# Attention and a Strassen MLP on one core: w_out's operand sums in place and two groups to a load, w_in's stores a round later, and another way to finish the last quarter

## Chip, cores, metric

The kernel runs on one NeuronCore of a Trainium2 chip. The metric is device microseconds (us) for one execution. The kernel before takes 911.48 us, the median of 8 runs (909.97 to 914.7).

## What is computed

A hashed attention feeds a two-layer MLP with a PReLU-like activation:

```python
# q, k, v: (4, 8, 768, 64); proj: (64, 6)
mask   = q_bucket[:, :, :, None] == k_bucket[:, :, None, :]   # sign bits of q @ proj and k @ proj
scores = where(mask, q @ k.T / 8, -1e9)
attn   = softmax(scores) @ v                                  # (4, 8, 768, 64)
x = attn.transpose(0, 2, 1, 3).reshape(3072, 512)
h = x @ w_in                                                  # w_in (512, 2048)
g = maximum(h, 0) + alpha * minimum(h, 0)
out = g @ w_out                                               # w_out (2048, 512), out (3072, 512)
```

## The kernel before

**Two paths.** `fast_path` computes everything and a flag; `general_path` runs only if the flag is set, which it is not here. Almost every instruction of an engine is put into a written-out order with `do(...)`. The DMA starts are not: a scheduler places them in the queue of SP (SyncE) by its own estimate of when they are due, and SP then takes them strictly in that order, so a DMA start that waits for a semaphore holds up all that are behind it.

**Attention** runs over 32 units (`u`), two for each of 16 pairs of heads, about 10.4 us each. A unit makes scores (`sc`), exponentials (`pt`), the product with v (`av`), the row sums (`sm`) and the quotient `x`, which goes to DRAM (`x_s`). Every second unit `turn` (line 669) transposes the next pair's q and k (`tp_q`, `tp_k`), whose tiles `qn` and `kn` are loaded by L500, and `vn` by L489. Beside that the weights are read (`raw`, L567), brought to shape, and grouped: `weight_group` stores finished groups of w_out into `w_out_r` and queues, for each of four groups of w_in, four sums (`one`, L638) and a store (`store`, L643: four DMA starts of 448 KB into `w_in_s`). `weight_sums(1)` takes one queued sum per unit, and the store at once behind the fourth sum.

**The MLP** is done by Strassen's scheme (Winograd's form: seven products instead of eight), two levels. For each of 4 batches there are 8 blocks `ff1` (`f_0` to `f_7`, tiles of w_in called `wi`) and 7 blocks `ff2` (`z_1` and so on, tiles of w_out called `wl`). Within a block PE does seven products in the order 1, 2, 5, 6, 3, 7, 4 (`Product.step`, banks a, b, c), and step 1 of the next block is put ahead of step 4 of this one, so PE's queue reads: step 1 of block n+1, step 4 of block n, steps 2, 5, 6, 3, 7 of block n+1, step 1 of block n+2, and so on. The tile `wi` of block n+2 (`load_w`, L827, two buffers) can be loaded only once step 4 of block n is done, and is needed at step 1 of block n+2.

**w_out's operand sums** are made in the first batch, beside its `ff1` blocks, in the two buffers that later hold `wl`. `load_out(n)` (L932) loads the four raw quarters of group n (512 KB) into the lower half of an eight-slot tile `wo`; `sum_out(n)` (L937) has VectorE (DVE) make four sums into the upper half, stores these (L938, 512 KB, into `w_out_s`) and calls `load_out(n + 2)`, which has to wait for that store to land since it reuses the tile. The loop over blocks `j` (L1147) calls `sum_out` for groups (0), (1, 2), (3), (4, 5), (6), (7) in the blocks j = 0 to 5, between the step 7 and the step 4 of that block. At j = 4 `largest` and `verdict` (L1034 to L1050) make the flag; PE has four tiny transposes there (`vd`).

**The end.** `ff2` adds the last product (p = 4) to the first (`m_1`). Its quarter "21" comes straight from PSUM: ScalarE (ACT) copies it (L980), DVE adds `m_1` (L974). `turn_last` (L1015) then transposes the last two output tiles on PE, copies them from PSUM on ACT (L1023) and stores them (L1025): `turn_last(0)` through SP, `turn_last(1)` in two parts through ACT's own DMA queue.

Of the kernel before, what the change touches and what calls it, by code (L numbers as in the profile page):

```python
# [8 lines left out]
F32 = mybir.dt.float32  # L9
# [3 lines left out]
ALU = mybir.AluOpType  # L13
# [393 lines left out]
def fast_path(  # L407
# [12 lines left out]
    nc = tc.nc  # L420
    P = 128
    B, H, S, D = q.shape
    NB = proj.shape[1]
    NTOK, DM = out.shape
# [6 lines left out]
    CH = 3  # L431
# [10 lines left out]
    do = tc.keep_in_program_order  # L442
    PE, DVE, ACT, POOL = nc.tensor, nc.vector, nc.scalar, nc.gpsimd
# [11 lines left out]
    out_v = out.rearrange("(b p c) d -> b c p d", p=P, c=NC)  # L455


    ident = const.tile([P, P], F32, name="ident")
# [12 lines left out]
    w_out_r = dram.tile([4, P, NI, DM // 2], F32, name="w_out_r")  # L471
    w_out_s = dram.tile([4, P, NI, DM // 2], F32, name="w_out_s")
# [149 lines left out]
    sums_due = []  # L622
# [25 lines left out]
        sums_due.append((store, ()))  # L648

    def weight_sums(count):  # L650
        while sums_due and (count or sums_due[0][0].__name__ == "store"):
            fn, x = sums_due.pop(0)
            count -= fn.__name__ == "one"
            fn(*x)


    def two_banks(name):
        return psum.tile([P, 2, 512], F32, name=name, tag="sc", bufs=3)
# [255 lines left out]
    H2, HK, HC = DM // 4, NI // 2, CW // 2  # L914
    w2, g2, m2, to_turn = {}, {}, {}, []

    def load_w2(b, n):

        if n < 7:
            t = late[0].tile([P, NI, 2 * H2], F32, name=f"wl{b}_{n}", tag="wl")  # L920
            m = SIDES[ORDER[n]][0]
            nc.sync.dma_start(t, w_out_r[m] if m < 3 else w_out_s[m - 3])
            for m, kh, dh in ((0, 0, 0), (1, 1, 0), (2, 1, 1), (21, 0, 1)):
                w2[b, n, m] = t.rearrange("p n (f i) -> p n i f", i=2)[:, kh * HK : (kh + 1) * HK, dh]

    w_o = {}

    def load_out(n):

        if n < NI:  # L930
            w_o[n] = late[0].tile([P, 8, DM // 2], F32, name=f"wo{n}", tag="wl")
            nc.sync.dma_start(w_o[n][:, :4], w_out_r[:, :, n].rearrange("m p d -> p m d"))  # L932

    def sum_out(n):
        w = w_o[n]
        for to, x, op, y in ((4, 3, ALU.add, 2), (6, 0, ALU.subtract, 3), (5, 4, ALU.subtract, 0), (7, 1, ALU.subtract, 5)):
            do(DVE.tensor_tensor(w[:, to], w[:, x], w[:, y], op=op))  # L937
        nc.sync.dma_start(w_out_s[:, :, n].rearrange("m p d -> p m d"), w[:, 4:])  # L938
        load_out(n + 2)

    def sides_g(b, n):
        t = g_m[b, SIDES[ORDER[n]][1]]
        for m, kh, ch in ((0, 0, 0), (1, 1, 0), (2, 1, 1), (12, 0, 1)):
            g2[b, n, m] = t[:, kh * HK : (kh + 1) * HK, ch * HC : (ch + 1) * HC]

    def sum_w2(b, n, *ms):

        if n < 7:
            for m in ms:
                x, op, y = {  # L950
                    3: (21, ALU.add, 2), 4: (3, ALU.subtract, 0), 5: (0, ALU.subtract, 21), 6: (1, ALU.subtract, 4),
                }[m]
                w2[b, n, m] = t = late[0].tile([P, HK, H2], F32, name=f"ws{b}_{n}_{m}", tag=f"ws{m}", bufs=1 + (m < 5))
                do(DVE.tensor_tensor(t, w2[b, n, x], w2[b, n, y], op=op))  # L954

    def sum_g2(b, n, *ms):

        if n < 7:
            for m in ms:
                x, y = {3: (12, 0), 4: (2, 3), 5: (2, 12), 6: (1, 4)}[m]  # L960
                g2[b, n, m] = t = late[0].tile([P, HK, HC], F32, name=f"gs{b}_{n}_{m}", tag=f"gs{m}", bufs=1 + (m < 5))
                do(DVE.tensor_tensor(t, g2[b, n, x], g2[b, n, y], op=ALU.subtract))  # L962

    def ff2(b, n):

        p = ORDER[n]
        acc = late[0].tile([P, 2, CW], F32, name=f"m{b}_{p}", tag={1: "m1", 5: "m5"}.get(p, "m"), bufs=1 if p in (1, 5) else 3)
        m2[b, p] = acc

        def add(to, x, *quarter):  # L970
            t, x = m2[b, to], m2[b, x]
            if quarter:
                t, x = (a[:, quarter[0], quarter[1] * HC : (quarter[1] + 1) * HC] for a in (t, x))
            do(DVE.tensor_tensor(t, t, x, op=ALU.add))  # L974

        def finish(c, x, more):
            i, jj = int(c[0]) - 1, int(c[1]) - 1
            dst = acc[:, i, jj * HC : (jj + 1) * HC]
            if more is None:
                do(ACT.copy(dst, x))  # L980
            else:
                do(DVE.tensor_tensor(dst, x, more, op=ALU.add))
            if p == 4:
                add(4, 1, i, jj)
            if c == "21":

                for to, x in {2: [(2, 1)], 6: [(1, 6)], 3: [(3, 5), (3, 1)], 7: [(1, 7), (5, 1)]}.get(p, []):
                    add(to, x)
                done = {2: (2, 0, 0), 3: (3, 0, 1), 7: (5, 1, 1), 4: (4, 1, 0)}.get(p)
                if done:  # L990
                    to_turn.append((b, *done))

        return Product(
            f"z{b}_{p}", HC, HK, lambda m, k: w2[b, n, m][:, k], lambda m, k: g2[b, n, m][:, k], finish,
        )

# [16 lines left out]
    def turn_last(n):  # L1013

        b, p, half, ch = to_turn.pop(0)  # L1015
        o = late[0].tile([P, CH, P, 2], F32, name=f"o_{p}", tag=("o", "m5")[n], bufs=2 - n)
        for ts in ((2,), (0, 1)) if n else ((0, 1, 2),):
            ps = two_banks(f"to{p}").rearrange("p a f -> p (a f)").rearrange("p (t i f) -> p t i f", i=2, f=P)
            for i in range(2):
                for t in ts:  # L1020
                    do(PE.transpose(ps[:, t, i], m2[b, p][:, i, t * P : (t + 1) * P], ident))
            ts = slice(ts[0], ts[-1] + 1)
            do(ACT.copy(o[:, ts].rearrange("p t f i -> p t i f"), ps[:, ts]))  # L1023
            dst = out_v[b, ch * CH : (ch + 1) * CH].rearrange("c p d -> p c d")
            (nc.scalar if n else nc.sync).dma_start(  # L1025
                dst[:, ts, half * 2 * P : (half + 1) * 2 * P], o[:, ts].rearrange("p t f i -> p t (f i)"),
            )


    top = const.tile([P, 4], F32, name="top")  # L1030
# [2 lines left out]
    def largest():  # L1033
        do(DVE.tensor_reduce(top[:, :2], mags, axis=mybir.AxisListType.X, op=ALU.max))  # L1034
        do(DVE.tensor_reduce(top[:, 2:3], wmax, axis=mybir.AxisListType.X, op=ALU.max))
        do(DVE.tensor_reduce(top[:, 3:4], alpha, axis=mybir.AxisListType.X, op=ALU.max))
# [102 lines left out]
    late = []  # L1139
    attn.close()  # L1140
    late.append(ctx.enter_context(tc.tile_pool(name="late", bufs=2)))
    load_out(0)
    load_out(1)
    blocks = [(b, what, n) for b in range(B) for what, count in (("1", NI), ("2", 7)) for n in range(count)]


    for j, (b, what, n) in enumerate(blocks):  # L1147
        n2 = n + 1 if what == "2" else 0 if n == NI - 1 else 7
        if n2 == 0:
            sides_g(b, 0)  # L1150
            sum_w2(b, 0, 3, 4)
        now.step(2) if j else now.step(6)
        if j == 0:
            now.step(3)
            now.step(7)
            now.step(2)
        now.step(22)
        if j == 4:
            largest()
        if 0 < n2 < 7:  # L1160
            sides_g(b, n2)
            sum_w2(b, n2, 3, 4)
        if n2 < 7:
            sum_g2(b, n2, 3, 4)
        if j:
            now.step(5)
            now.step(6)
            now.step(3)
            sum_w2(b, n2, 6)
            now.step(7)  # L1170
            sum_w2(b, n2, 5)
            sum_g2(b, n2, 5)
        if j == 4:
            verdict()
        for n_out in [(0,), (1, 2), (3,), (4, 5), (6,), (7,)][j] if j < 6 else ():
            sum_out(n_out)
        if what == "1":
            load_w(b * NI + n + 2)
            if n >= NI - 2:
                load_w2(b, n - NI + 2)  # L1180
        else:
            load_w2(b, n + 2)
            if b + 1 < B:
                if n == 0:
                    load_x(b + 1)
                if n == 6:
                    for m in range(4):
                        sum_x(b + 1, m, DVE)
        if j + 1 < len(blocks):
            turn_out()  # L1190
        else:
            turn_last(0)
        before = now
        if j + 1 < len(blocks):
            b1, what1, n1 = blocks[j + 1]
            now = ff1(b1, n1) if what1 == "1" else ff2(b1, n1)
            now.step(1)
        before.step(4)
        if n2 < 7:
            sum_g2(b, n2, 6)  # L1200
# [29 lines left out]
```

## Time and profile before

| what | us |
|---|---|
| median of 8 runs | 911.48 |
| the profiled execution, its whole time | 913.63 |
| its span, first to last instruction | 911.8 |
| PE (TensorE) busy | 888.5 (97%) |
| VectorE (DVE) busy | 756.1 (83%) |
| ScalarE (ACT) busy | 410.5 (45%) |
| attention, up to the first `ff1` product | 0 to 352.9 |
| first batch's `ff1` blocks | 352.9 to 432.0 |
| last matmul product ends, span ends | 903.5, 911.8 |

The mean granted clock of TensorE is 0.996 of full speed over the span. HBM moves 146 GB/s over the span; in the stretch from 355 to 425 us, where w_out's sums are made, 232 GB/s. "L848" is line 848 of the kernel; tiles are given by their names without numbers. PE is busy nearly all the time, so the few stretches in which it is not are what there is to read; a busy share of another engine says little by itself.

### The profile page before, as it was taken

To read this page: it belongs to the slowest core of one execution; us is meant where nothing else is said; L and a number is where in the kernel's file an instruction comes from. 1 tells how busy PE (TensorE), PEld (TensorE's weight loads), DVE (VectorE), ACT (ScalarE), POOL (GpSimd) and SP (SyncE) were. 2 spreads that over 40 slices of the span, in tenths; PEclk is the share of its full clock that TensorE was granted. 3 is DMA by queue.
4 is the path that set the end of the run, shared out by engine and by line. 5 is a ranking of instruction groups with operands and counts; after the bars stand their busy time and mean duration, and the time that the engine had idled before them with its cause. 6 is when DMAs were issued, how large, how long until landed. Compare 5 with 4: busy or idle time off the path is not lost.

```text
span 911.8 us, 15639 instructions
## 1 busy us (share of the span) xinstructions
PE 888.5 (97%) x5885; PEld 590.9 (65%) x5885; DVE 756.1 (83%) x1353; ACT 410.5 (45%) x735; POOL 88.3 (10%) x178
## 2 busy tenths in 40 slices
PE   7999999999999999989999999999999999999996
PEld 3444444444444445546998556998556998556996
DVE  4888898988998997887889667989667989768985
ACT  6888888888888873222111222111222112222111
POOL 1222222222223221000000000000000000000000
PEclk9999999999999999999999999999999999999999
DMA  8787887698788764767333534333535333531242
GB/s 219 188 203 167 212 214 202 171 259 230 172 226 201 181 170 143 242 221 267 132 112 114 159 119 155 128 116 112 164 113 168 115 129 98 173 103 40 93 141 72
DMA packets 138053, 146.88 MB, mean 161 GB/s; under 512 B 78304, under 2 KB 126192, under 8 KB 134384
## 3 DMA queue, kind: packets, MB, share of 16 engines
q1 hardware_dynamic: 127248, 132.42, 47.0%
q0 software_dynamic: 8704, 12.58, 8.6%
q8 instruction: 48, 0.79, 0.4%
q10 hardware_dynamic: 2016, 0.79, 0.3%
q14 instruction: 37, 0.30, 0.1%
HBM read 104.87 MB, written 28.31 MB: 146 GB/s over the span
## 4 chain that ended last, share of the span: by engine, by line
PE 56%; DMA 4%; DVE 2%; POOL 0%; ACT 0%; issue 0%; SPq 0%; DVEq 0%; ACTq 0%; POOLq 0%
PE f_6a L848 2%; PE z_4a L848 2%; PE z_6a L848 2%; PE z_7a L848 2%; PE z_3a L848 2%; PE z_5a L848 2%; PE z_2a L848 2%; PE z_1a L848 2%; PE f_7a L848 2%; PE f_0a L848 2%; PE f_1a L848 2%; DMA w_out_s<-wo 2%; PE f_5a L848 2%; PE f_2a L848 2%; PE f_4a L848 2%; PE f_3a L848 2%
## 5 line engine op out<-in xcount | busy, mean ns | idle before, releaser
L733 ACT ACTIVATE pt<-sc 128x768 f32<-128x768 f32 x192 | 152.7, 813 | 49.5 <-PE sc L728 47.3
L728 PE MATMUL sc<-qT,kT 64*128 64x384 f32 x768 | 155.1, 482 | 0.0
L761 PE MATMUL av<-pt,vn 128*32 128x384 f32 (+1 forms) x1536 | 130.6, 488 | 2.8 <-DVE x L802 2.7
L761 PEld LDWEIGHTS av<-pt,vn 128*32 128x32 f32 x1536 | 46.6, 109 | 78.4 <-issue 68.9
L728 PEld LDWEIGHTS sc<-qT,kT 64*128 64x128 f32 x768 | 68.1, 188 | 34.4 <-issue 34.2
L898 DVE TENSOR_TENSOR g<-g,g 128x384 f32<-128x384 f32 x128 | 68.4, 555 | 2.2
L728 PE MATMUL sc<-qb,kb 64*128 64x384 bf16 x384 | 63.0, 324 | 2.5 <-ACT kb L716 1.0
L743 POOL DMA_DIRECT2D accp<-pt x32 | 38.5, 1204 | 188.9 <-issue 101.0
L962 DVE TENSOR_TENSOR gs<-g,gs 128x768 f32<-128x768 f32 x56 | 53.4, 953 | 1.0
L962 DVE TENSOR_TENSOR gs<-g 128x768 f32<-128x768 f32 x56 | 53.3, 952 | 0.0
L954 DVE TENSOR_TENSOR ws<-wl 128x512 f32<-128x512 f32 x56 | 38.5, 688 | 17.7 <-DMA wl<-w_out_s 16.5
L894 DVE SCALAR_TENSOR_TENSOR g<-h,alpha 128x384 f32<-128x384 f32 x32 | 19.7, 617 | 29.2 <-ACT h L887 29.2
L728 PEld LDWEIGHTS <-kb 64*128 64x128 bf16 x384 | 19.4, 94 | 34.2 <-issue 12.1
L705 ACT ACTIVATE qb<-hs,hb 32x384 bf16<-32x384 f32 x62 | 35.6, 574 | 1.1
L748 DVE TENSOR_TENSOR accd<-accd,pt 128x768 f32<-128x768 f32 x32 | 30.7, 958 | 3.3
L751 DVE TENSOR_TENSOR accd<-accd,accp 128x768 f32<-128x768 f32 x32 | 30.7, 958 | 2.8 <-DMA accp<-pt 1.7
L799 DVE STREAM_TRANSPOSE dn<-rr 128x384 f32<-128x384 f32 x32 | 18.5, 578 | 17.4 <-POOL rr L797 17.4
L742 DVE TENSOR_TENSOR accp<-pt,pt 128x768 f32<-128x768 f32 x32 | 30.4, 952 | 2.0 <-ACT pt L733 2.0
L747 DVE TENSOR_TENSOR accd<-pt,pt 128x768 f32<-128x768 f32 x32 | 30.4, 949 | 0.4 <-ACT pt L733 0.4
L974 DVE TENSOR_TENSOR m<-m,m 128x768 f32<-128x768 f32 (+1 forms) x40 | 28.4, 709 | 1.9 <-ACT m L980 1.2
L797 POOL COPY rr<-rr 32x6 f32<-32x6 f32 x64 | 27.6, 431 | 2.6
L716 ACT ACTIVATE kb<-hs,hb 64x384 bf16<-64x384 f32 (+1 forms) x47 | 27.2, 578 | 0.6
(334 smaller groups left out, 1794.4 us busy)
## 6 DMA issues: line engine op xcount, KB each, us to landing
wi<-w_in_s SPq DMA_DIRECT2D x32, 896.0 KB, 4.9
wl<-w_out_s SPq DMA_DIRECT2D x16, 1024.0 KB, 4.8
accp<-pt POOLq DMA_DIRECT2D x32, 384.0 KB, 5.1
wl<-w_out_r SPq DMA_DIRECT2D x12, 1024.0 KB, 4.9
raw<-in_moe_w_out_dram SPq DMA_DIRECT2D x16, 512.0 KB, 4.8
raw<-in_moe_w_in_dram SPq DMA_DIRECT2D x16, 512.0 KB, 4.4
w_in_s<-wsi SPq DMA_DIRECT2D x16, 448.0 KB, 5.2
vn<-in_v_dram SPq DMA_DIRECT2D x16, 384.0 KB, 6.3
```

The lines of the kernel that those rows point to most:

```text
L705: do(ACT.activation(bits["q", pi][D * s : D * s + 32, cols], ps["q"][c : c + 32, half, :CW], AF.Sign, bias=hb[c : c + 32],))
L728: do(PE.matmul(sc[:, s, :CW], what["k", pi][r, ks], what["q", pi][r, qs], start=first, stop=not first,))
L733: do(ACT.activation(pt[:, :, :CW], sc[:, :, :CW], AF.Exp, scale=SCALE / DOWN))
L742: do(DVE.tensor_tensor(accp[u], p(u, 0), p(u, 1), op=ALU.add))
L743: nc.gpsimd.dma_start(accp[u], p(u, 2), accum_op=ALU.add)
L748: do(DVE.tensor_tensor(accd[u], accd[u], p(u, 5), op=ALU.add))
L751: do(DVE.tensor_tensor(accd[u], accd[u], accp[u], op=ALU.add))
L761: do(PE.matmul(av[u][D * s + t : D * s + t + 32, :w], nat["v", pi][:, s, kc * D + t : kc * D + t + 32], prob[u, kc][:, s, :w], start=(kc = ...
L848: do(PE.matmul(self.ps[bank], self.left(left, k), self.right(right, k), start=start and k == 0, stop=k == self.nk - 1, skip_group_check=no ...
L898: do(DVE.tensor_tensor(new_g(b, to)[:, i], g_m[b, x][:, i], g_m[b, y][:, i], op=ALU.subtract))
L954: do(DVE.tensor_tensor(t, w2[b, n, x], w2[b, n, y], op=op))
L962: do(DVE.tensor_tensor(t, g2[b, n, x], g2[b, n, y], op=ALU.subtract))
```

## The change

Four edits, in the order of the diff.

1. `weight_sums` no longer takes the store together with the fourth sum; the store is taken at the next unit's call.
2. `w_out`'s sums overwrite their operands (the four quarters of a group become its four sums, in the slots 2, 3, 0, 1, and `load_w2` reads `w_out_s` through the new order). A tile now has room for two groups, loaded by two DMA starts one after the other, so four groups are loaded at the start, and groups 4 and 5 (then 6 and 7) are loaded when both groups of a tile are summed and stored. The groups are summed as (0), (1), (2), (3, 4), (5), (6), (7) in the blocks j = 0 to 6.
3. In `ff2` the quarter that comes from PSUM is, for p = 4, added to `m_1` by DVE straight from PSUM; ACT's copy is gone there.
4. `turn_last` copies one half-row set `i` at a time, and for the very last tile groups the six transposes so that only the two cells that the last quarter touches are in the second part.

```diff
     def weight_sums(count):
-        while sums_due and (count or sums_due[0][0].__name__ == "store"):
+
+        while sums_due and count:
             fn, x = sums_due.pop(0)
             count -= fn.__name__ == "one"
             fn(*x)
...
-            nc.sync.dma_start(t, w_out_r[m] if m < 3 else w_out_s[m - 3])
+            nc.sync.dma_start(t, w_out_r[m] if m < 3 else w_out_s[(2, 0, 3, 1)[m - 3]])
...
     def load_out(n):
         if n < NI:
-            w_o[n] = late[0].tile([P, 8, DM // 2], F32, name=f"wo{n}", tag="wl")
-            nc.sync.dma_start(w_o[n][:, :4], w_out_r[:, :, n].rearrange("m p d -> p m d"))
+            t = late[0].tile([P, 2, 4, DM // 2], F32, name=f"wo{n}", tag="wl")
+            for i in range(2):
+                nc.sync.dma_start(t[:, i], w_out_r[:, :, n + i].rearrange("m p d -> p m d"))
+                w_o[n + i] = t[:, i]
     def sum_out(n):
         w = w_o[n]
-        for to, x, op, y in ((4, 3, ALU.add, 2), (6, 0, ALU.subtract, 3), (5, 4, ALU.subtract, 0), (7, 1, ALU.subtract, 5)):
+        for to, x, op, y in ((2, 3, ALU.add, 2), (3, 0, ALU.subtract, 3), (0, 2, ALU.subtract, 0), (1, 1, ALU.subtract, 0)):
             do(DVE.tensor_tensor(w[:, to], w[:, x], w[:, y], op=op))
-        nc.sync.dma_start(w_out_s[:, :, n].rearrange("m p d -> p m d"), w[:, 4:])
-        load_out(n + 2)
+        nc.sync.dma_start(w_out_s[:, :, n].rearrange("m p d -> p m d"), w)
+        if n % 2:
+            load_out(n + 3)
...
         def finish(c, x, more):
             i, jj = int(c[0]) - 1, int(c[1]) - 1
             dst = acc[:, i, jj * HC : (jj + 1) * HC]
-            if more is None:
+            if more is not None:
+                do(DVE.tensor_tensor(dst, x, more, op=ALU.add))
+                if p == 4:
+                    add(4, 1, i, jj)
+            elif p == 4:
+                do(DVE.tensor_tensor(dst, x, m2[b, 1][:, i, jj * HC : (jj + 1) * HC], op=ALU.add))
+            else:
                 do(ACT.copy(dst, x))
-            else:
-                do(DVE.tensor_tensor(dst, x, more, op=ALU.add))
-            if p == 4:
-                add(4, 1, i, jj)
...
     def turn_last(n):
...
-        for ts in ((2,), (0, 1)) if n else ((0, 1, 2),):
-            ps = two_banks(f"to{p}").rearrange("p a f -> p (a f)").rearrange("p (t i f) -> p t i f", i=2, f=P)
+        dst = out_v[b, ch * CH : (ch + 1) * CH].rearrange("c p d -> p c d")[:, :, half * 2 * P : (half + 1) * 2 * P]
+        goes = [([(t, i) for i in range(2) for t in range(CH)], slice(0, CH))]
+        if n:
+            goes = [([(2, 0), (2, 1), (0, 0), (1, 0)], slice(2, CH)), ([(0, 1), (1, 1)], slice(0, 2))]
+        for cells, ts in goes:
+            ps = two_banks(f"to{p}").rearrange("p a f -> p (a f)").rearrange("p (i t f) -> p i t f", i=2, f=P)
+            for t, i in cells:
+                do(PE.transpose(ps[:, i, t], m2[b, p][:, i, t * P : (t + 1) * P], ident))
             for i in range(2):
-                for t in ts:
-                    do(PE.transpose(ps[:, t, i], m2[b, p][:, i, t * P : (t + 1) * P], ident))
-            ts = slice(ts[0], ts[-1] + 1)
-            do(ACT.copy(o[:, ts].rearrange("p t f i -> p t i f"), ps[:, ts]))
-            dst = out_v[b, ch * CH : (ch + 1) * CH].rearrange("c p d -> p c d")
-            (nc.scalar if n else nc.sync).dma_start(
-                dst[:, ts, half * 2 * P : (half + 1) * 2 * P], o[:, ts].rearrange("p t f i -> p t (f i)"),
-            )
+                t = [c[0] for c in cells if c[1] == i]
+                if t:
+                    t = slice(min(t), max(t) + 1)
+                    do(ACT.copy(o[:, t, :, i], ps[:, i, t]))
+            (nc.scalar if n else nc.sync).dma_start(dst[:, ts], o[:, ts].rearrange("p t f i -> p t (f i)"))
...
     load_out(0)
-    load_out(1)
+    load_out(2)
...
-        for n_out in [(0,), (1, 2), (3,), (4, 5), (6,), (7,)][j] if j < 6 else ():
+        for n_out in [(0,), (1,), (2,), (3, 4), (5,), (6,), (7,)][j] if j < 7 else ():
             sum_out(n_out)
```

In the queue of SP, as the scheduler lays it out, the change moves the following. Of the first two groups of w_in, the first of a store's four DMA starts keeps its place ahead of the loads of qn, vn and kn, and the other three go behind the loads of kn, `x_s` and `raw`; the two later groups keep their places. In the first batch's `ff1` blocks the order was

`wo0 wo1 | wi2 | s0 | wo2 | wi3 | s1 s2 | wo3 wo4 | wi4 | s3 | wo5 | wi5 | s4 s5 | wo6 wo7 | wi6 | s6 | wl0 | wi7 | s7 | wl1`

(s for a store of sums, wi2 for the w_in tile of block `f_2`) and becomes

`wo0 wo1 wo2 wo3 | s0 | wi2 | s1 | wi3 | wo4 wo5 | wi4 | s2 | wi5 | s3 s4 | wo6 wo7 | wi6 | s5 | wl0 | wi7 | s6 | x_0 | next wi | s7 | x_1 x_2 | wl1`.

The order on PE and on GpSimd does not change. On DVE, counted by block, four sums leave block 1 and four come into block 6; in between each four is made for another group than before.

## The prediction

> **What bounds the kernel now.** I read the page's busy shares first (PE 97%), so a gain must come from the few microseconds in which PE stands still or runs slowly. The list of PE's waits says where these are. Columns: engine, line, releaser, us in total, times, longest.
>
> ```profile
> PE tp_k L669 <- DMA kn<-in_k_dram: 3.0, 2, 1.6
> ...
> PE f_6a L848 <- DMA wi<-w_in_s: 2.0, 1, 2.0
> PE f_4a L848 <- DMA wi<-w_in_s: 1.6, 1, 1.6
> PE vd L1041 <- DVE top L1034: 1.4, 1, 1.4
> ```
>
> The largest of the rest (`av` waiting for DVE's x, 2.7 in five) is in work that the change leaves alone. PE's timeline places the waits (start, us, what, in brackets the idle time before it):
>
> ```profile
> 137.73 0.84 PE L669 MATMUL tp_k<-ident,kn 128*128 128x128 f32 x6 [1.41 <-DMA kn<-in_k_dram]
> ```
> ```profile
> 202.01 0.85 PE L669 MATMUL tp_k<-ident,kn 128*128 128x128 f32 x6 [1.57 <-DMA kn<-in_k_dram]
> ```
> ```profile
> 386.98 1.56 PE L848 MATMUL f_4a<-x,wi 128*128 128x384 f32 x4 [1.56 <-DMA wi<-w_in_s]
> ...
> 397.69 0.60 PE L1041 MATMUL vd<-ident,top 128*1 128x128 f32 x4 [1.41 <-DVE top L1034]
> ...
> 409.44 2.33 PE L848 MATMUL f_6a<-x,wi 128*128 128x384 f32 x4 [2.04 <-DMA wi<-w_in_s]
> 411.56 2.42 PE L848 MATMUL f_5a<-x,wi 128*128 128x384 f32 x4
> 413.82 1.45 PE L848 MATMUL f_6b<-x,wi 128*128 128x384 f32 x4
> ```
>
> The last three rows hold a second loss: starts of such products are 1.29 us apart everywhere else, here 2.12 and 2.26, so 0.83 + 0.97 = 1.80 us more. The windows show why: the granted clock is 0.50 from 410.5 to 413.5. After the idle times of 1.41, 1.57 and 1.56 us it stayed 1.00.
>
> SP's own timeline shows both causes.
>
> ```profile
> 120.88 4.24 SPq L643 DMA_DIRECT2D w_in_s<-wsi  x4
> 125.22 1.35 SPq L489 DMA_DIRECT2D vn<-in_v_dram  x1
> 126.67 2.06 SPq L500 DMA_DIRECT2D qn<-in_q_dram  x2
> 128.82 4.09 SPq L500 DMA_DIRECT2D kn<-in_k_dram  x2
> ```
> ```profile
> 377.05 1.75 SPq L932 DMA_DIRECT2D wo<-w_out_r  x2
> 378.99 0.36 SPq L827 DMA_DIRECT2D wi<-w_in_s  x1
> ...
> 399.16 1.76 SPq L932 DMA_DIRECT2D wo<-w_out_r  x2
> 401.01 0.46 SPq L827 DMA_DIRECT2D wi<-w_in_s  x1
> ```
>
> In attention, four DMA starts of a w_in store take 4.24 us ahead of the loads of q and k, and kn is late. In the first batch's blocks, two `wo` loads go just ahead of a `wi` load: asked one by one, the `wi` issued at 378.99 landed after 7.9 us and that at 401.01 after 8.4, where the median of the later batches is 4.6. What is allowed follows from block 2: `wi` issued at 360.93, its product at 367.19 without a wait, so 6.26 us from issue to use.
>
> **The change, part by part.** The sum is made against the profiled execution (span 911.8, whole time 913.63, that is 1.83 outside the span) and put on the median of the runs, 911.48, which is 2.15 below that execution.
>
> *w_in's stores.* Three of four starts leave the place ahead of q and k in the first two groups, the two that line up with the two `tp_k` waits. Then kn is issued about 3 x 1.05 us (the median start) earlier, plus what the full queue cost: its two starts took 4.09 us here and 2.29 at 143.38 with no store ahead. Together some 5 us; kn landed 1.41 late. The three starts come behind the `raw` load. They hold up a `raw` and an `x_s`; `raw` is used ten microseconds (a unit) later and lands in 4.5. In the second group `wi1` now waits for such a store to land (5.2): SP has that time, it stood waiting from 200.4 to 205.2. So both waits go: -1.41 - 1.57 = -2.98. Bounds: 0, if kn is still late, and -2.98, since nothing else of PE's idle time hangs on it. The `av` waits stay.
>
> *w_out's sums, what goes.* No group waits for the store two groups before it, and the load pairs move. The waits at f_4a, vd and f_6a and the slow clock behind the last are removed as they stand: -1.56 - 1.41 - 2.04 - 1.80 = -6.81.
>
> *w_out's sums, what comes.* First, block 2. Four `wo` loads (2.1 MB) instead of two start at 356.97, and in SP's queue `wi2` now stands behind the store of group 0. That store waits for DVE's sums: 360.68 + 1.55 = 362.2, so `wi2` is issued at about 362.65, not 360.93, and must land by 367.19. At the shortest, 4.9 (what this load took before) gives 367.55 and a wait of 0.4. At the longest, 8.4 gives 371.05 and a wait of 3.9. For the value: the loads move some 0.34 MB per us (315 to 387 GB/s in the half-microsecond slices from 358.5 to 361), so of 2.1 MB begun at 358.0 about 0.5 are open at 362.65; with the store's 0.5 and its own 0.9 that is 1.9 MB, where the load that took 7.9 had 1.65 ahead and in it. It is nearest to that row: 7.7, landing at 370.35. I take +3.1. Idle for 3.1 us is more than the 2.04 that brought the half clock: +1.80 (bounds 0 and 1.80).
>
> Then, block 3: `wi3` stands behind the store of group 1, 1 us later than before, but PE is 3 us later by then: 0. Blocks 4 and 5: the `wo` pair for groups 4 and 5 goes when store 1 has landed, before block 2 is through, and only stores follow `wi4` and `wi5`, as behind the `wi` at 369.96, which landed in 5.7: 0. The flag: DVE no longer stands 2.42 and 2.50 us for `wo` ahead of `largest`; by its rows it gets there 0.2 after PE: +0.2 (0 to 0.4).
>
> Block 6: the pair for groups 6 and 7 waits for store 3, which lands about 6.4 us (as the store at 370.66) after it is issued, that is close to the start of block 4's step 4, 1.7 and 1.3 us ahead of `wi6`. Before f_4a the same pair was 1.9 and 0.6 ahead and cost 7.9; with the second load 0.7 further on I take 7.4, 1.1 late: +1.1 (0, if 6.26 is kept; 8.4 gives 2.1). Block 7: `wl0` (1 MB) waits for store 5, which comes behind the flag's work, so that it is issued 1 to 2 us ahead of `wi7` instead of 3.2: between 5.6 (as before) and 7.9, I take 6.9: +0.6 (0 to 1.6).
>
> Block 8 on: `wl1` goes behind `x_1`, `x_2` and store 7, some 5 us later than before; it is asked for by DVE at 438.63, 13 us after it landed (425.7): hidden; without that cover the next is z_2c, which starts at 442.29, just behind DVE, so any more delay would reach PE. The four sums new in block 6 (1.55) fit DVE's idle 1.31 there and its 0.23 and 1.21 before: 0.
>
> Added: 3.1 + 1.8 + 0.2 + 1.1 + 0.6 = 6.8. Against -6.81 the edit is worth nothing, with bounds of -6.4 (only 0.4 comes) and +4.8 (3.9 + 1.8 + 0.4 + 2.1 + 1.6 and a second slow clock, 1.8).
>
> [...]
>
> *The last quarter and the last turn.* PE's last product ends at 903.48. Before: ACT copy 0.32 at 903.51, DVE add 0.36 at 903.87, two transposes 904.28 to 904.72, ACT copy of 512 columns 0.61 at 904.75, store at 905.39. Now DVE adds from PSUM (0.35, as L982) at 903.52, the transposes end by 904.36. But ACT has more to do first: of the four early transposes (done 903.91) a copy of 384 columns (0.50, between 0.39 for 256 and 0.61 for 512), one of 128 (0.28), then its DMA start 0.37, all in order, to 905.06; the last copy, 256 columns, 0.39, to 905.47. The store is issued at 905.5: +0.1. Bounds: -0.6, if ACT doesn't stand behind its DMA start, and +0.3. In the other three batches the saved ACT copy ends nothing.
>
> Sum: -2.98 - 0.0 + 0.1 = -2.9. Time: 911.48 - 2.9 = 908.6.
>
> **The rivals.** *The third block hardly waits.* If the DMA engines serve `wi2` within about 6 us of its issue (a wait of 1.5, clock kept) and 0.5 is lost later, 2.0 is added: 911.48 - 2.98 - 6.81 + 2.0 + 0.1 = 903.8. For it: two `wo` loads are then nearly through. Against: no `wi` behind a `wo` pair landed in under 7.9.
>
> *Nothing is left.* kn is late even so, because the stores' bytes (1.8 MB) still go through the same engines in the same unit: 911.48 + 0.0 + 0.1 = 911.6. For it: `qn` and `kn` landed after 6.5 to 8.0 us in that unit, 3.8 to 5.5 in the next. Against: an earlier issue of 5 us against a lateness of 1.5.
>
> *Slower: `wi` behind the sums in SP's queue.* Blocks 2, 6 and 7 each wait as long as the worst row allows, 3.9 + 2.1 + 1.6, the flag 0.4, and each brings the slow clock, 3 x 1.8: 13.4, so 911.48 - 2.98 - 6.81 + 13.4 + 0.1 = 915.2. It decides from 11.5 us added on (beyond 913.3). For it: all three stand behind stores or loads in one queue. Against: the waits at f_4a and `tp_k` of this size left the clock whole.
>
> **How the numbers follow.** Forecast 0.52, third block short 0.27, nothing left 0.13, slower 0.08. The forecast's own range is 906 to 911, from block 2's wait between 1.5 and 3.9 and the clock. The range 903.0 to 912.5 leaves out the tails of the second and the fourth case. About 0.2% (1.8 us) is what a measurement of this kernel can tell from no change: faster is below 909.7, slower above 913.3. Faster: 0.41 of the forecast and 0.27, 0.68. Same: 0.11 and 0.13, 0.24. Slower: 0.08.
>
> **What would show it.** No PE idle time before `tp_k` near 137 and 202, kn landing before 136. An idle time of about 3 us before f_2a near 367, put down to `wi`, with the clock at 0.50 behind it; none before f_4a; 1 us before f_6a, less before f_7a. The last store issued at the same distance from PE's last product. Wrong it would be if f_2a starts within 1 us of its time, if a wait appears at z_2c or z_2a for `wl1`, or if `tp_k` still waits.

## The result, and the profile after

The changed kernel takes 909.03 us, the median of 15 runs (905.86 to 910.91), beside 912.73 us for 43 runs of the kernel before on the same chip. The ratio is 0.9958 with a 95% interval of 0.9948 to 0.9968: 3.8 us less (2.9 to 4.7 on 911.5 us), which is more than the 0.2% that can be told from no change. The forecast was 908.6, a gain of 2.9. Two more executions of the changed kernel, 908.70 (the profiled one) and 911.82, leave the median at 909.03.

The list of PE's waits of the kernel after (engine, line, releaser, us in total, times, longest) starts so:

```profile
PE av L762 <- DVE x L803: 4.5, 7, 1.2
PE f_2a L849 <- DMA wi<-w_in_s: 2.6, 1, 2.6
PE nil L516 <- DVE hb L520: 1.2, 1, 1.2
```

The rows that led the list before (`tp_k`, f_6a, f_4a, `vd`) are no longer among its longest. A wait before f_2a is new, and the `av` row has grown from 2.7 in five to 4.5 in seven. PE's timeline of the kernel after (start, us, what, idle time before it) shows the same places:

```profile
135.78 0.49 PE L670 MATMUL tp_k<-ident,kn 128*128 128x128 f32 x3
...
197.98 0.82 PE L670 MATMUL tp_k<-ident,kn 128*128 128x128 f32 x6
...
252.39 4.09 PE L762 MATMUL av<-pt,vn 128*32 128x385 f32 x48 [1.15 <-DVE x L803]
...
367.67 1.56 PE L849 MATMUL f_2a<-x,wi 128*128 128x384 f32 x4 [2.57 <-DMA wi<-w_in_s]
369.06 1.45 PE L849 MATMUL f_1a<-x,wi 128*128 128x384 f32 x4
```

Both `tp_k` rows have no idle time before them; f_2a waits 2.57 us. The product behind it starts 1.39 us later, near the usual 1.29, so the half clock that was forecast there did not come in this execution. The windows of the kernel after say it outright (stretch, us, busy time of PE, weight load, DVE, ACT, POOL, the granted clock, DMA share, GB/s):

```profile
365.00:368.00 3.00, 0.43 (x2) 0.30 (x2) 2.50 (x6) 0.48 (x1) 0.00 (x0) 1.00 0.33 136
368.00:371.00 3.00, 3.00 (x11) 1.71 (x10) 0.59 (x2) 0.93 (x2) 0.00 (x0) 1.00 0.48 165
```

SP's timeline of the kernel after shows how both parts of the diff arrive in its queue:

```profile
120.16 0.58 SPq L643 DMA_DIRECT2D w_in_s<-wsi  x1
120.83 2.09 SPq L500 DMA_DIRECT2D qn<-in_q_dram  x2
122.98 0.78 SPq L489 DMA_DIRECT2D vn<-in_v_dram  x1
123.86 1.23 SPq L500 DMA_DIRECT2D kn<-in_k_dram  x2
...
126.77 3.80 SPq L643 DMA_DIRECT2D w_in_s<-wsi  x3
```
```profile
354.71 2.02 SPq L934 DMA_DIRECT2D wo<-w_out_r  x4
360.44 0.36 SPq L942 DMA_DIRECT2D w_out_s<-wo  x1
360.84 0.50 SPq L828 DMA_DIRECT2D wi<-w_in_s  x1
...
395.96 0.91 SPq L934 DMA_DIRECT2D wo<-w_out_r  x2
398.37 0.33 SPq L828 DMA_DIRECT2D wi<-w_in_s  x1
```

The starts of kn are through at 125.1 instead of 132.9. In the blocks, `wi2` goes out only behind four `wo` loads and a store.

The span cut at three of PE's rows gives an account by stage: attention up to f_0a's step 6 (the steps 1 and 5 of `f_0` run inside it, from 345.5 us on in before, so 352.9 is not the first `ff1` product of all), the first batch's `ff1` blocks up to the first product of z_1a, the rest up to the start of the last z_4a product, and the end from there. The first two lines are the two kernels, the others are the experiments below.

| profiled kernel | attention | blocks | rest | end | span |
|---|---|---|---|---|---|
| before | 352.89 | 76.41 | 472.63 | 9.87 | 911.8 |
| after | 350.64 | 72.13 | 473.37 | 10.66 | 906.8 |
| stores_only | 349.92 | 73.46 | 472.32 | 9.70 | 905.4 |
| sums_only | 352.64 | 74.27 | 472.34 | 9.65 | 908.9 |
| tail_only | 352.63 | 74.78 | 472.94 | 10.35 | 910.7 |
| psum_add_only | 352.38 | 74.29 | 472.32 | 9.91 | 908.9 |
| sums_ahead | 352.24 | 71.60 | 472.56 | 9.9 | 906.3 |
| two_ahead | 350.31 | 70.98 | 473.03 | 10.28 | 904.6 |
| late_wi | 348.82 | 72.87 | 472.34 | 10.17 | 904.2 |
| ahead_old_tail | 350.71 | 73.45 | 472.32 | 9.7 | 906.2 |
| all_old_tail | 349.38 | 71.19 | 472.46 | 10.2 | 903.2 |
| best | 349.55 | 70.88 | 472.33 | 10.1 | 902.9 |

After against before: -2.25 in attention, -4.28 in the blocks, +0.74 in the rest, +0.79 at the end, -5.0 in all. That is 1.2 more than the runs show. The profiled execution of before is a long one, 2.15 above its median; it holds the 1.80 that the half clock cost, which many executions lack (see the last section).

### The profile page after: what moved, and what is told of

Its sections match the earlier page's. It is cut to its first block, busy times and chain, and to the rows that moved or that the text cites. A ratio compares the mean times of both kernels' runs of the same rounds, so it can differ in the third digit from the quotient of the medians.

```text
span 906.8 us, 15639 instructions
## 1 busy us (share of the span) xinstructions
PE 886.9 (98%) x5885; PEld 591.1 (65%) x5885; DVE 757.3 (84%) x1353; ACT 408.7 (45%) x733; POOL 88.3 (10%) x178
## 4 chain that ended last, share of the span: by engine, by line
PE 56%; DVE 4%; DMA 2%; issue 1%; POOL 0%; ACT 0%; ACTq 0%; DVEq 0%; POOLq 0%
PE z_4a L849 2%; PE f_2a L849 2%; PE z_3a L849 2%; PE z_5a L849 2%; PE z_6a L849 2%; PE f_5a L849 2%; PE f_0a L849 2%; PE z_2a L849 2%; PE f_6a L849 2%; PE f_3a L849 2%; PE z_7a L849 2%; PE f_1a L849 2%; PE f_4a L849 2%; PE z_1a L849 2%; PE f_7a L849 2%; PE z_2c L849 1%
## 5 line engine op out<-in xcount | busy, mean ns | idle before, releaser
L752 DVE TENSOR_TENSOR accd<-accd,accp 128x768 f32<-128x768 f32 x32 | 30.7, 958 | 5.3 <-DMA accp<-pt 4.4
```

Source lines behind the costliest of these rows:

```text
L752: do(DVE.tensor_tensor(accd[u], accd[u], accp[u], op=ALU.add))
```

## The experiments

The first theory was that of the prediction: the stores give the gain, the sums take about as much as they give, because `wi2` stands behind four loads and a store, and the end is neutral. The first four runs take the edits apart and mend the suspected wait. Each ratio is against the kernel before on the same chip, with its 95% interval; us are that ratio on 911.5.

**stores_only**: the kernel before with edit 1 alone.

```diff
-        while sums_due and (count or sums_due[0][0].__name__ == "store"):
+        while sums_due and count:
```

> The kernel before with the first edit alone (w_in's stores a unit later). The page of the changed kernel has no tp_k wait any more, but its av waits for DVE's x rose from 2.7 to 4.5 us in all, and DVE stood 3.8 us for accp there, where it did not before. My theory: both come from this edit (the moved stores and the two wi loads behind them now run beside the accp transfers). Then here: no tp_k wait (-2.98), av waits about 4.5 (+1.8), attention ends some 1.2 us earlier, and the time is 1 to 1.5 us below the kernel before. Rival: the av waits have nothing to do with it (chance, or the other edits): av waits 2.7 and the time 3.0 us lower. Second rival: the wait at tp_k stays: no gain.

908.96 us (8 runs), ratio 0.9968 (0.9957 to 0.9979): -2.9. The `tp_k` waits are gone. The first line of PE's waits of this kernel is, as in the kernel after, a longer `av` row:

```profile
PE av L761 <- DVE x L802: 3.8, 6, 1.2
PE f_7a L848 <- DMA wi<-w_in_s: 1.3, 1, 1.3
```

So the growth of `av` comes with the stores and not with the sums. The theory's time, 1 to 1.5 us below, lies outside the interval (1.9 to 3.9 below): the place of the wait came as expected, its price did not.

**sums_only**: the kernel before with edit 2 alone.

> The kernel before with the second edit alone (w_out's sums in place, two groups to a load, seven blocks). My theory: the waits at f_4a, vd and f_6a go (5.0 us) with the slow clock behind them (1.8), and a wait of 2.6 before f_2a comes: 4.2 us lower where the clock keeps its speed. tp_k waits stay at 3.0, attention ends where it did. Rival: part of the 3.7 us of the whole change that this would leave too large (4.2 + 1.2 is more than 3.7) is lost elsewhere, so that this edit alone gives 2 to 3 us.

910.65 us (11 runs), ratio 0.9995 (0.9979 to 1.0011): -0.5, no change that can be told. PE's waits of this kernel:

```profile
PE f_2a L848 <- DMA wi<-w_in_s: 3.2, 1, 3.2
PE tp_k L669 <- DMA kn<-in_k_dram: 3.1, 2, 1.6
PE av L761 <- DVE x L802: 2.6, 5, 0.8
PE f_7a L848 <- DMA wi<-w_in_s: 1.3, 1, 1.3
```

The waits at f_4a, `vd` and f_6a are gone, and f_2a and f_7a wait 4.4 in their place. `av` is as it was before. Both the theory (4.2 lower) and the rival (2 to 3 lower) missed: they took the 5.0 of one execution for what goes, 2.6 for the wait at f_2a, and nothing for f_7a.

**tail_only**: the kernel before with edits 3 and 4.

> The kernel before with the third and fourth edit alone (last quarter added by DVE from PSUM, last turn copied in halves). My theory from the sum: the last store is issued 0.1 us later after PE's last product than in the kernel before (1.91 there), time +0.1, no difference that can be told. Rival: it is what lengthened the end in the changed kernel's profile, where the last store came 2.23 us after the product and the end 9.1 instead of 8.3 us after it: +0.3 to +0.8.

911.1 us (12 runs), ratio 0.9996 (0.998 to 1.0013): nothing that can be told. In its trace the last store goes out 3.78 us behind the start of PE's last product, as in the kernel after, against 3.46 in before.

**two_ahead**: the kernel after, with `wi2` issued ahead of the second pair of `wo` loads and of the store of group 0 (its DMA start is put into the written-out order). `wi3` then goes ahead of the store of group 1 too.

```diff
     load_out(0)
-    load_out(2)
...
+        if what == "1":
+            load_w(b * NI + n + 2)
+            if j == 0:
+                load_out(2)
         for n_out in [(0,), (1,), (2,), (3, 4), (5,), (6,), (7,)][j] if j < 7 else ():
             sum_out(n_out)
         if what == "1":
-            load_w(b * NI + n + 2)
```

> The changed kernel, with only two of the four wo loads ahead of the tile wi2 and that ahead of the first store in SP's queue; the other two follow behind wi2. My theory: the wait of 2.6 us at f_2a goes and nothing takes its place (the second pair is asked for only in block 2): 2.5 us below the changed kernel, 6.2 below the kernel before. Rival: the wait comes from the bytes of the first batch as such, and moves to f_3a or f_4a: no difference from the changed kernel.

904.59 us (5 runs), ratio 0.9921 (0.9907 to 0.9934): -7.2, the best of the first four. SP's timeline of this kernel shows `wi2` at 358.35, two loads ahead of it instead of four and a store:

```profile
354.39 0.92 SPq L934 DMA_DIRECT2D wo<-w_out_r  x2
358.35 0.33 SPq L828 DMA_DIRECT2D wi<-w_in_s  x1
358.73 0.98 SPq L934 DMA_DIRECT2D wo<-w_out_r  x2
359.81 0.70 SPq L942 DMA_DIRECT2D w_out_s<-wo  x1
```

PE's timeline of it has no idle time at f_2a:

```profile
364.61 1.45 PE L849 MATMUL f_2a<-x,wi 128*128 128x384 f32 x4
```

**sums_ahead**: the same order with edit 2 alone, that is, two_ahead without edits 1, 3 and 4. It tells whether the f_2a wait is what eats the gain of the sums.

> The kernel before with the second edit alone, and wi2 with two wo loads ahead of the rest as in two_ahead. sums_only gave -0.5 us (-1.9 to +1.0) with a wait of 3.2 at f_2a. My theory: the wait at f_2a was all that ate the edit's gain, so here it is gone and the time is 3 to 4.5 us below the kernel before; with the stores' 2.9 that makes two_ahead's 7.2. Rival: two_ahead was fast because the edits help each other (PE earlier in attention moves the blocks' traffic): here 1 to 2 us only.

907.85 us (12 runs), ratio 0.9959 (0.9943 to 0.9975): -3.7, where sums_only gave -0.5. PE's waits of this kernel no longer name f_2a:

```profile
PE tp_k L669 <- DMA kn<-in_k_dram: 3.0, 2, 1.6
PE av L761 <- DVE x L802: 2.5, 5, 0.8
PE f_7a L848 <- DMA wi<-w_in_s: 1.5, 1, 1.5
```

The stores alone (-2.9) and these sums (-3.7) make -6.6, close to two_ahead's -7.2. The intervals of sums_ahead and sums_only, 0.9943 to 0.9975 and 0.9979 to 1.0011, do not overlap, and the two kernels differ only in this order.

The new order is not free of waits. It asks for the second pair of `wo` loads later, so that the pair for groups 4 and 5 now goes out 1.5 to 2.1 us ahead of `wi4` (7.9 us in the kernel after). In the two of the five kernels with this order in which the pair is nearest, f_4a waits: 0.99 us in ahead_old_tail (1.5 ahead) and 1.13 in all_old_tail (1.8 ahead). In the other three (2.0 to 2.1 ahead) it does not. So the rival in two_ahead's expectation, that the wait moves on to f_4a, holds in part in some executions; that the pair is the cause is argued from the order, not shown by a run. PE's timeline of ahead_old_tail:

```profile
384.67 1.56 PE L849 MATMUL f_4a<-x,wi 128*128 128x384 f32 x4 [0.99 <-DMA wi<-w_in_s]
```

**late_wi**: a second theory, for the `av` waits. In the kernel after SP issues the first two `wi` loads (0.9 MB each, not needed before 345 us) right behind the three store starts that were moved, as SP's timeline of after shows:

```profile
189.70 3.78 SPq L643 DMA_DIRECT2D w_in_s<-wsi  x3
193.52 4.00 SPq L828 DMA_DIRECT2D wi<-w_in_s  x2
```

`accp` is a sum of two parts of the exponentials, made by DVE, onto which a DMA on GpSimd's queue adds a third part; DVE uses the result at L752. DVE's timeline of after has four waits for it, at 137, 199, 211 and 221 us, where the kernel before has none (before waits for `accp` only at 22.6 and 278.9, 1.44 and 0.22 us). Two of the four are just behind that burst:

```profile
210.69 0.96 DVE L752 TENSOR_TENSOR accd<-accd,accp 128x768 f32<-128x768 f32 x1 [1.69 <-DMA accp<-pt]
...
221.16 0.96 DVE L752 TENSOR_TENSOR accd<-accd,accp 128x768 f32<-128x768 f32 x1 [0.60 <-DMA accp<-pt]
```

The experiment is the kernel after with the two loads eight units later (their DMA starts are put into the written-out order too).

```diff
         if u == HW + 2:
+            load_x(0)
+        if u == HW + 10:
             load_w(0)
             load_w(1)
-            load_x(0)
```

> The changed kernel, with the first two wi loads (1.8 MB, needed only in the MLP) eight units later than in unit 18, where they run right behind the moved w_in stores. DVE stood for accp 0.71, 1.69 and 0.60 us at 199, 211 and 221 us of the changed kernel's profile, and PE's waits for DVE's x went from 2.7 to 4.5 us. My theory: the wi loads slow the accp transfers: here the waits for accp at 211 and 221 are gone (0.5 or less), av waits are 2.7 or less, and the time is about 1.5 us below the changed kernel's, 5 below the kernel before. Rival: the three moved starts of the store do it: the accp waits stay at 3 us and the time is the changed kernel's.

905.99 us (5 runs), ratio 0.9941 (0.9928 to 0.9954). DVE's waits at 211 and 221 are gone (those at 137 and 200, beside the stores themselves, stay), and the first line of PE's waits is back to what it was before the change:

```profile
PE av L762 <- DVE x L803: 2.6, 5, 0.8
```

The `av` rows at 241 and 252 us (0.55 and 1.15) are missing, and attention is 1.8 shorter than in after. As the intervals of the two ratios overlap, the size of the gain in time stays open; the place of the wait does not. The other profiles agree: the wait at 211 is 1.7 to 2.2 us in the four kernels with moved stores and early `wi` loads, and 0.2 or nothing in the three with late ones. The transfer itself says the same: the `accp` issued in that unit (at 201.35 in after) landed after 9.0 to 9.5 us in the four, after 6.5 to 7.5 in the three.

It was no faster before the change. In before the `accp` issued at 203.04 landed after 9.1 us, that is at 212.1, but its reader came later still, at the end of a unit that held the wait at `tp_k` and took 12.4 us, where the units beside it took 10.0 and 10.1:

```profile
213.11 0.96 DVE L751 TENSOR_TENSOR accd<-accd,accp 128x768 f32<-128x768 f32 x1
```

So the change did not slow this transfer; it brought the reader forward, and the wait at `tp_k` had hidden how late the data came.

**ahead_old_tail** and **all_old_tail**: two_ahead with the old code of the last quarter and the last turn, without and with late_wi's edit. **best**: two_ahead with late_wi's edit, the new tail, and the first of the two last stores through SP's queue.

```diff
-            (nc.scalar if n else nc.sync).dma_start(dst[:, ts], o...
+            (nc.scalar if ts.start == 0 and n else nc.sync).dma_start(dst[:, ts], o...
```

> The kernel two_ahead (changed kernel, wi2 and two wo loads ahead of the rest) without the third and fourth edit. In three profiles with these edits the span's end comes 10.3 to 10.7 us after the start of PE's last product, in three without them 9.7 to 9.9, and the stretch of the MLP from z_1 on is some 0.5 us longer. Theory from these: the two edits cost about 1 us, so 8 below the kernel before. Rival (my sum): they are worth nothing, 7 below, as two_ahead.

905.74 us (5 runs), ratio 0.9929 (0.9916 to 0.9941).

> two_ahead with the late wi loads and without the third and fourth edit. If the gains add: -7.2 for two_ahead, -1.5 for the late loads, -1 if the last edits cost: 8.5 to 9.7 below the kernel before. If the av waits are not due to the loads: 7 to 8 below.

904.71 us (5 runs), ratio 0.9921 (0.9909 to 0.9934).

> two_ahead with the late wi loads, and with the first of the two last stores started by SP instead of ACT, so that ACT goes on to the last copy at once. In the changed kernel's profile the last copy began 0.45 us after ACT was ready for it, behind the DMA start: so the last store is issued 1.8 us after PE's last product instead of 2.23, and the time is 0.4 us below that of two_ahead with the late loads alone, some 9 below the kernel before. Rival: the end is set by how long the last transfers take, not by when they are issued: no gain from it.

904.68 us (6 runs), ratio 0.9922 (0.9908 to 0.9936). No one of the three stands apart from two_ahead: neither the tail nor the late loads add to its gain by anything that can be told. What was expected if all gains add up (8 below for ahead_old_tail, 8.5 to 9.7 for all_old_tail, 9 for best) lies outside the intervals, -7.7 to -5.4, -8.3 to -6.0 and -8.4 to -5.8. A part of the reason shows in the profiles: in all_old_tail and best the late `wi` loads, now at 294 us, meet another `accp`. DVE waits 0.50 and 0.69 us for it at 306 us, where no kernel with early loads waits (nor does late_wi), and PE's `av` waits are 3.2 and 3.3 instead of late_wi's 2.6. The blocks of the three last 70.9 to 73.5 us in the table above with the same order of loads, so the scatter of single executions is as large as what is sought. In `best` the last store goes out 3.03 us behind the start of PE's last product, the earliest of all, and the span still ends 10.1 behind it.

**psum_add_only**: the kernel before with edit 3 alone.

> The kernel before with the third edit alone: DVE adds the last quarter from PSUM, the last turn as before. My theory: ACT's copy (0.32) and a hand-over leave the chain behind PE's last product, so the last store is issued 3.1 us after that product's start instead of 3.46 (the changed kernel: 3.78), and the time falls by 0.3 at most, which can't be told. Rival: DVE's read from PSUM is slower to start, no earlier store.

910.7 us (12 runs), ratio 0.9997 (0.9984 to 1.001). ACT's timeline of this kernel, whose last product starts at 898.99:

```profile
901.21 0.37 ACTq L1027 DMA_DIRECT2D out_dram<-o  x1
901.63 0.61 ACT L1025 COPY o<-to 128x512 f32<-128x512 f32 x1 [0.45 <-PE to L1023]
902.27 0.39 ACTq L1027 DMA_DIRECT2D out_dram<-o  x1
```

The last store is issued 3.28 behind the product, 0.18 earlier than the 3.46 of before: the saved ACT copy is worth that much here, and not the 0.36 expected; ACT's own DMA start (901.21 to 901.58) stands just ahead of the last copy. A difference of 0.2 us is below what the times can tell.

## Why the prediction held, point by point

**w_in's stores, -2.98.** Right in mechanism and place: both `tp_k` waits went, and alone the edit gave -2.9 (-3.9 to -1.9). One sentence in it was wrong: "The `av` waits stay." They grew by 1.8 in the profile of after, by 1.1 in that of stores_only. The step that failed is the look at what else lands in those units: it followed `raw`, `x_s` and `wi`, all of SP's queue, and not `accp` on GpSimd's, which landed only just ahead of its reader as long as the wait at `tp_k` held the reader back. That the time still fell by the full 2.9 is not explained by the two rows, -2.98 and +1.1 to +1.8; the interval is wide enough for both. Attention shows what is left. The five kernels with the old stores end it at 352.2 to 352.9, the four with the new stores and early `wi` loads at 349.9 to 350.7 (2.2 less by the means), the three with late loads at 348.8 to 349.6 (3.3 less). So about a microsecond was given back. The DVE rows put the wait at 211 down to the `wi` loads.

**w_out's sums, 0.** Right in the sum: -0.5 (-1.9 to +1.0) alone. The mechanism was right where it counted most, the wait at f_2a; that the sum came out near 0 was partly luck, as terms that were too large stood on both sides.

What goes: f_4a, `vd` and f_6a were put at 5.01, from one execution. PE's timeline of psum_add_only, whose blocks are those of before, has four waits, smaller but with one more:

```profile
386.29 1.56 PE L848 MATMUL f_4a<-x,wi 128*128 128x384 f32 x4 [1.40 <-DMA wi<-w_in_s]
396.62 0.60 PE L1043 MATMUL vd<-ident,top 128*1 128x128 f32 x4 [1.03 <-DVE top L1036]
407.03 1.56 PE L848 MATMUL f_6a<-x,wi 128*128 128x384 f32 x4 [0.69 <-DMA wi<-w_in_s]
417.53 1.56 PE L848 MATMUL f_7a<-x,wi 128*128 128x384 f32 x4 [1.21 <-DMA wi<-w_in_s]
```

In stores_only the four are 0.99, 0.82, 0.35 and 1.34, in tail_only 1.75, 0.83, 1.04 and 1.20. So the three that were priced at 5.01 measured 2.2 to 3.6 there, 3.5 to 4.8 with f_7a. Of the four only before, whose profile has the half clock ahead of it, has no wait at f_7a.

What comes: f_2a waits 2.57 in after, 3.16 in sums_only, where 3.1 was forecast. That `wi2` would stand behind the store and the four loads was right; in after it was issued 10.20 after the start of the blocks (9.76 forecast) and its product ran 6.8 after the issue, in sums_only 9.6 and 8.0; 7.7 was taken. The +1.80 of half clock did not come in the profiled executions of after and sums_only; the mean clock of their runs, 0.996 or less in 6 of 17 and in 3 of 11, says that such a loss comes in some (last section). The +1.1 at f_6a did not come in either: in after the `wo` pair went out 2.4 us ahead of `wi6`, not 1.7 and 1.3, and the load landed after 4.9, inside the 6.26 allowed. The +0.6 at f_7a is 0 in after, 1.28 in sums_only, 0.8 in late_wi. The flag's transposes show no wait in after (+0.2 forecast).

So neither of the two 1.80 that were set against each other is a fixed cost. (The prediction read the half clock from 410.5 on; narrower windows show it from 410.1 to 413.5.) Without them, the waits that go are 3.5 to 5.0 (mean 4.4 over before, stores_only, tail_only and psum_add_only, f_7a counted), and those that come are 2.6 to 4.4: about -1 us, within the interval of sums_only. sums_ahead shows that the edit is worth -3.7 (-5.2 to -2.3) once `wi2` doesn't pay for it; its blocks are 2.6 us shorter than the mean of the three kernels with the old order and no half clock.

**The last quarter, +0.1.** A little worse in the trace, and nothing in time. ACT's timeline of after, whose last product starts at 896.14:

```profile
898.40 0.66 ACT L1036 COPY o<-to 128x384 f32<-128x384 f32 x2 [1.15 <-PE to L1031]
899.09 0.37 ACTq L1037 DMA_DIRECT2D out_dram<-o  x1
899.51 0.38 ACT L1036 COPY o<-to 128x256 f32<-128x256 f32 x1 [0.45 <-ACT o L1036]
899.92 0.39 ACTq L1037 DMA_DIRECT2D out_dram<-o  x1
```

The order on ACT is as forecast: two copies, a DMA start, the last copy behind it. The store goes out 3.78 after the product began, against 3.46: +0.32, at the upper bound given. In the stage table the rest is 0.6 to 1.1 us longer in after, tail_only and two_ahead than in late_wi and best, which have the same edits 3 and 4 and the 472.3 of the old code: in the first three the last `wl` load landed after 6.7 to 6.9 us, against 5.2 to 5.6 in before, stores_only and sums_only, and PE's z_4a waited 0.3 to 0.5 for it. The end is 0.2 to 0.8 longer in the kernels with both edits than in before, but all_old_tail has 10.2 with the old code. Why these differ is not settled.

**The rivals.** "The third block hardly waits" fell with the 2.57 of f_2a, though the kept clock that it counted on was there in the profile. "Nothing is left" fell with the `tp_k` rows: kn is in time. The stores' bytes did meet `accp`, which in the units of the two stores landed after 8.2 and 8.1 us (7.3 and 7.5 before) and let DVE wait 0.77 and 0.71; no kernel with the old stores waits there. "Slower" fell because in after neither f_6a nor f_7a waits, and the wait at f_2a did not bring the half clock in the profile. `wl1` behind `x_1` and `x_2` stayed hidden, as argued: PE has no wait at z_2c or z_2a.

Stores -2.9, sums -0.5 and tail -0.4 add up to the -3.8 measured for the whole, against -2.9 forecast; none of the three is known to better than a microsecond.

## What to carry to other kernels

A load that PE waits for should be put into the queue ahead of loads that only prepare later work: moving the start of `wi2` past two loads and a store (and `wi3` past a store) turned an edit of no worth that can be told into 3.7 us, and the kernel from 0.9958 to 0.9921. When a wait is removed, look at the DMA queues of all engines for the transfer that lands just in time behind it, not only at the queue in which the change is made. And read the size of a wait from several executions before it enters a sum: the same waits were 3.5 to 5.0 us in four kernels with the same code there.

## What the runs showed of the hardware

**The half clock came in some executions and not in others.** Two stretches with about the same or a longer idle time behaved differently. The window of before that holds the stretch behind f_6a's 2.04 us of idle time:

```profile
410.00:413.50 3.50, 3.50 (x8) 1.76 (x7) 1.64 (x5) 0.48 (x1) 0.00 (x0) 0.51 0.42 142
```

and the windows of sums_only around f_2a, idle for 3.16 us up to 370.26:

```profile
368.00:371.00 3.00, 0.74 (x2) 0.49 (x3) 2.49 (x6) 0.00 (x0) 0.00 (x0) 1.00 0.10 41
371.00:374.00 3.00, 3.00 (x11) 1.80 (x10) 0.34 (x1) 0.96 (x2) 0.00 (x0) 1.00 0.51 175
```

In before the clock was halved for 3.4 us, from 410.1 to 413.5; in sums_only it stayed whole. So the length of the idle time alone did not decide it; what did is not shown. PE's end shows that the time at which the clock falls varies: there PE has nothing left to do, and in the twelve profiles the granted clock falls to 0.50 at times between 2.8 us (sums_ahead) and 5.8 us (stores_only) behind the end of the last product. In before it is 5.0 us (908.5), in after 4.8 (902.5). The mean clocks of the whole profiles, 0.997 in sums_ahead and 0.999 in stores_only, agree: an estimate from them, with all the loss at the end, puts the fall 2.0 to 3.8 us and 5.4 to 7.2 us behind.

The runs give the share. From there to the end of the span it lowers the mean clock by 0.001 to 0.003 in the twelve profiles (0.0018 in before, 0.0024 in after); one stretch like that of before takes another 0.5 x 3.4 / 912 = 0.002. So a mean of 0.996 or less is more than the end explains, 0.998 or more leaves no room for such a stretch, and 0.997 can be either. Of 59 runs of the kernel before beside the experiments, 17 had 0.996 or less (median 912.8 us), 22 had 0.997 (911.6) and 20 had 0.998 or more (911.0). Of the changed kernel, with its wait at f_2a, 6 of 17 had 0.996 or less, of sums_only 3 of 11, of late_wi none of 5, of the three other kernels with the blocks of before 4 of 32; of the five kernels that have `wi2` ahead, and no PE wait for a load above 1.6 us in the blocks, none of 33. Where in the span such a run loses its clock is not recorded. So a loss of this size came in a part of the executions, and a forecast for these kernels should carry it as a chance, on both sides of the sum.

**`accp`, a DMA on GpSimd's queue, landed late beside bursts on SP's.** `accp` (384 KB) takes 5.1 us from issue to landing at the median of before. Beside the two 896 KB `wi` loads it took 9.1 us in before and 9.2 in after, where three 448 KB store starts stood just ahead of them; with the loads moved away (late_wi, all_old_tail, best), 6.5 to 7.5. DVE waited 1.69 us for it in after, and not at all in before, where the reader came later.
